# A job's scaled result leaves behind the next branch, and the short job runs its first layer by halves

## The chip, the cores and the metric

The kernel runs on one core of one Trainium2 chip. It uses TensorE (matmuls, into PSUM), VectorE, ScalarE, GpSimd (here mostly to issue gathers and scatters by a list of row numbers) and SyncE (which issues the plain DMA loads). The metric is the device time of one execution in microseconds. Every engine has its own queue of instructions and its own sequencer; the engines wait for each other by semaphores, and at a branch in the program each engine compares and jumps for itself.

## The reference, cut to what matters

Three layers follow each other: attention with a window and some global tokens, a dense layer of three products with a maximum, and a mixture of experts. Only the last is touched:

```python
logits = x @ w_gate                      # 1152 tokens, 8 experts
expert_idx = np.argmax(logits, axis=1)
...
h = np.maximum(np.einsum('ecd,edf->ecf', disp, w1), 0.0)   # 512 -> 1024
y = np.einsum('ecf,efd->ecd', h, w2)                       # 1024 -> 512
...
out[i] = gate_w[i] * y[expert_idx[i], pos[i]]              # at most 288 tokens per expert
```

So every token goes through the two layers of its expert, and its row is scaled by the gate's weight and put at its place in `out`. Rows over the capacity of 288 stay zero.

## The kernel before

The first 265 us compute attention, the dense layer, the routing and the fullest expert (job 0). What is left is cut into **jobs** of at most 128 tokens of one expert, the fullest first. Their number and sizes are known only at run time, so the program is a nest of branches, written by the recursion `jobs` (L1209): job j runs, then a branch (L1214) looks at the count of job j + 1. Over 32 tokens, the next full job follows; else a second branch inside the Else (L1217) either runs the **short job** `small` (L990), for 1 to 32 tokens, or ends. With these inputs four full jobs run (1 to 4), and job 5 is a short one.

A full job (`job`, L984) has 24 matmuls of the first layer (`first_tile`, L890, into two PSUM banks of `ACC`), ScalarE's Relu (L895), four transposes for each of the two halves of the hidden layer (`hidden`, L911, copied out at L912 and L913), and 24 matmuls of the second layer (`second`, L924). In between, by hand-written places, ScalarE and VectorE split the next job's weights into two parts (L840, L841), the next job's tokens are transposed (`xprep`, L811 to L816), the next count is loaded into a register on each engine (L1200), a hint on the coming branch is given (L982), and GpSimd gathers the tokens of the job after next (L799). SyncE loads the weights for the job after next as the splits free their buffers; where such a job doesn't exist, the load moves nothing.

At the end of `second` ScalarE scales the 128 x 512 result by the gate's weights into `y` (L930), and GpSimd scatters `y` to the rows of `out` (L931). Both are written ahead of the branch. All scatters write the same tensor `out`; the framework that orders the instructions makes each of them wait until the one before has landed.

The short job works with weights as they were loaded: `small` has 16 small matmuls for the first layer (L998, four groups of 32 rows, 256 columns each), one Relu by ScalarE (L1003), two transposes (L1005), a copy by VectorE (L1006), eight one-column operations by VectorE that make row numbers and gate weights for four column blocks (L1011, L1012), 32 small matmuls for the second layer (L1017), a scaling by ScalarE (L1019) and a scatter by GpSimd (L1020). After it the program ends: SyncE waits for all DMAs, and the engines meet (L1311).

In the trace a 4-byte matmul of the source shows as two records.

Of the kernel before, what the change touches and what calls it, by code (L numbers as in the profile page):

```python
# [7 lines left out]
F32 = mybir.dt.float32  # L8
# [5 lines left out]
AF = mybir.ActivationFunctionType  # L14
# [5 lines left out]
P = 128  # L20
# [3 lines left out]
DM = H * D  # L24
# [10 lines left out]
NJ = NU_ + 1  # L35
# [15 lines left out]
def tile_block(ctx: ExitStack, tc: tile.TileContext, qk, qg, v, vo, vg, w123, w_out, w_gate, w1, w2, consts, out):  # L51
    nc = tc.nc
# [65 lines left out]
    ident = cst[:, 0:P]  # L118
# [527 lines left out]
    k = 0  # L646
# [8 lines left out]
    ps_x = ctx.enter_context(tc.tile_pool(name="ps_x", bufs=2, space=PSUM))  # L655
    ps_y = ctx.enter_context(tc.tile_pool(name="ps_y", bufs=2, space=PSUM))
# [10 lines left out]
    k = 0  # L667
# [100 lines left out]
    def drive(main, sides=()):  # L768

        t, due = 0, [[g, 0] for g in sides]  # L770
        for _ in main:
            t += 1
            for d in due:
                if d[0] is not None and d[1] <= t:
                    n = next(d[0], None)
                    d[0], d[1] = (None, 0) if n is None else (d[0], t + n)
        for d in due:
            if d[0] is not None:
                for _ in d[0]:
                    pass  # L780

    def chain(*gens):
        for g in gens:
            yield from g() if callable(g) else g
# [7 lines left out]
    TOK = [(0, P), (P, P), (2 * P, CAP - 2 * P)]  # L792
# [25 lines left out]
    XS = []  # L818
# [5 lines left out]
    def raw_of(j, k):  # L824

        r = rw0[k % 3] if j == 0 and k < 5 else raw2[k]
        return r if k < 4 else r.rearrange("p (i f) -> p i f", i=2)
# [87 lines left out]
    def second(j, t, a0):  # L915

        hh, hl = H0, H0[:, :, CAP + 32 :]
        _, _, w2h, w2l = WS[j % 2]
        nt = TOK[t][1]
        py = ps_y.tile([P, DM], F32, tag="py", name="py")  # L920
        i = 0
        for a, w_, c0 in ((hh, w2h, 0), (hh, w2l, 0), (hl, w2h, 0), (hh, w2h, 4), (hh, w2l, 4), (hl, w2h, 4)):
            for c in range(c0, c0 + 4):
                nc.tensor.matmul(py[0:nt], lhsT=a[:, c, a0 : a0 + nt], rhs=w_[:, c], start=i == 0, stop=i == 23)  # L924
                i += 1
                if i < 24:
                    yield
        i_ = IDS[j][0:nt, t]
        y = pB.tile([P, DM], F32, tag="y", bufs=2, name="y")
        nc.scalar.mul(y[0:nt], py[0:nt], i_[:, 2:3])  # L930
        nc.gpsimd.indirect_dma_start(  # L931
            out=out, out_offset=bass.IndirectOffsetOnAxis(ap=i_[:, 1:2].bitcast(I32), axis=0),
            in_=y[0:nt], in_offset=None, bounds_check=NT - 1, oob_is_err=False)
        yield


    FEW = 2 * P
# [21 lines left out]
            in_=y[0:32], in_offset=None, bounds_check=NT - 1, oob_is_err=False)  # L959
        yield  # L960

    ACC = [None, None]

    def accumulators():
        a = [ps_mm.tile([P, 512], F32, tag="mm", name=f"acc{i}") for i in range(3)] + [ps_m4.tile([P, 512], F32, tag="mm", name="acc3")]
        ACC[:] = [a[0:2], a[2:4]]

    def tile_of(j, place):

        yield place  # L970
        xprep(j, 0, ps_x, "px")
        gather_tile(j + 2, 0)

    def counts(j, place):

        yield place
        count_of(j)

    def hint(j, place):

        yield place
        tc.mark_branch_hint_location(f"job{j}", nreg[j] > SMALL, [mybir.EngineType.PE, mybir.EngineType.Activation, mybir.EngineType.DVE, mybir.EngineType.Pool])  # L982

    def job(j):  # L984

        more = j + 1 < NJ
        sides = [counts(j + 1, 6), splits(j + 1, ((0, 0), (1, 3), (2, 13), (3, 19), (4, 25), (5, 31), (6, 35), (7, 39))), tile_of(j + 1, 30), hint(j + 1, 20)] if more else []
        drive(chain(first_tile(j, 0, ACC[j % 2]), second(j, 0, 0)), [hidden(P, (18, 28)), *sides])

    def small(j):  # L990

        sx = pB.tile([P, 512], F32, tag="hs", bufs=2, name="sx")
        sh = pB.tile([P, 512], F32, tag="hs", bufs=2, name="sh")
        ph = ACC[j % 2][0]
        for k in range(4):
            for g in range(4):
                r = slice(32 * g, 32 * g + 32)
                nc.tensor.matmul(ph[r, 0:256], lhsT=XS[0][:, k], rhs=raw_of(j, k)[:, 256 * g : 256 * g + 256], start=k == 0, stop=k == 3)  # L998
        hr = sx[:, 0:256]
        hT_ = sh[:, 0:256].rearrange("p (i t) -> p i t", i=2)  # L1000
        pt = ps_x.tile([P, 2, P], F32, tag="px", name="st")
        py = ps_y.tile([P, P], F32, tag="py", name="sy")
        nc.scalar.activation(hr, ph[:, 0:256], AF.Relu)  # L1003
        for i in range(2):
            nc.tensor.transpose(pt[:, i], hr[:, i * P : i * P + P], ident)  # L1005
        nc.vector.tensor_copy(hT_, pt)  # L1006
        i_ = IDS[j][0:SMALL, 0]
        io, g4 = sh[:, 256:257].bitcast(I32), sh[:, 257:258]
        for q in range(4):
            r = slice(32 * q, 32 * q + 32)  # L1010
            nc.vector.tensor_copy(g4[r], i_[:, 2:3])  # L1011
            nc.vector.tensor_scalar(io[r], i_[:, 1:2].bitcast(I32), 4.0, float(q), op0=ALU.mult, op1=ALU.add)  # L1012
        for i in range(2):
            for k in range(4):
                for q in range(4):
                    r = slice(32 * q, 32 * q + 32)
                    nc.tensor.matmul(py[r], lhsT=hT_[:, i, 32 * k : 32 * k + 32], rhs=raw_of(j, 4 + k)[:, i, q * P : q * P + P], start=i == 0 and k == 0, stop=i == 1 and k == 3)  # L1017
        y = pB.tile([P, DM], F32, tag="y", bufs=2, name="ys")
        nc.scalar.mul(y[:, 0:P], py, g4)  # L1019
        nc.gpsimd.indirect_dma_start(  # L1020
            out=out.rearrange("t (q c) -> (t q) c", q=4), out_offset=bass.IndirectOffsetOnAxis(ap=io, axis=0),
            in_=y[:, 0:P], in_offset=None, bounds_check=4 * NT - 1, oob_is_err=False)
# [5 lines left out]
    ereg, nreg, nsp = [None] * NJ, [None] * NJ, [None] * NJ  # L1028
# [75 lines left out]
    def splits(j, places):  # L1104
        t = 0
        for k, p in places:
            yield p - t
            t = p
            split(j, k)
# [82 lines left out]
    def regs(*jobs):  # L1192

        a, b = jobs[0], min(jobs[-1], NJ - 1) + 1
        if a < b:
            for i, (to, top) in enumerate(((ereg, NE - 1), (nsp, NT))):
                _, to[a:b] = nc.values_load_multi_w_load_instructions(order[0:1, i, a - 1 : b - 1], engines=(mybir.EngineType.SP,), min_val=0, max_val=top)
# [11 lines left out]
    def jobs(j):  # L1209
        if j > 1:  # L1210
            regs(j + 2, j + 2)
        job(j)
        if j + 1 < NJ:
            with tc.If(nreg[j + 1] > SMALL, label=f"job{j + 1}") as c:  # L1214
                jobs(j + 1)
            with c.Else():
                with tc.If(nreg[j + 1] > 0):  # L1217
                    small(j + 1)

    drive(  # L1220
        chain(first_wide(0, CAP, ps_w), second(0, 0, 0), second(0, 1, P), second_few(0, 2)),
# [93 lines left out]
```

## Time and profile before

| what | us |
|---|---|
| median of three runs | 329.09 |
| the three runs | 330.13, 329.09, 327.28 |
| the profiled execution | 327.76 |
| its span, from the first to the last instruction | 325.9 |
| TensorE busy in the span | 309.4 (95%) |
| VectorE, ScalarE, GpSimd busy | 230.6, 183.6, 148.3 |

The span is what the profile's rows cover; the device time of the same execution is 1.86 us longer. All times of rows are counted from the span's start. A busy share is a mean over stages with different limits: what a change in one stage is worth is read in that stage.

### The profile page before, as it was taken

What the parts mean: (1) busy time and instruction counts of PE and PEld (TensorE: products, weight loads), DVE (VectorE), ACT (ScalarE), POOL (GpSimd) and SP (SyncE); (2) the same over time, 40 slices, a digit from 0 to 9 for tenths busy, and PEclk for the clock granted to TensorE, in tenths of its full rate; (3) what the DMA queues carried; (4) which work ended last, traced back from release to release, by engine and by line L of the source; (5) the groups of instructions that cost most, each with busy time, mean ns of one, the idle gap of its engine ahead of it and who ended that gap; (6) DMA issues with size and microseconds to landing.
All of it is one profiled execution on the core that took longest, in us unless ns stands there. A gap on an engine that the chain in (4) does not pass through costs nothing. (4 is left out here: it accounts for less than half of the span.)

```text
span 325.9 us, 8459 instructions
## 1 busy us (share of the span) xinstructions
PE 309.4 (95%) x3145; PEld 257.7 (79%) x3145; DVE 230.6 (71%) x593; ACT 183.6 (56%) x470; POOL 148.3 (45%) x164
## 2 busy tenths in 40 slices
PE   7999878999999999999999999999999999999982
PEld 2444646777777899999999999999899777888762
DVE  1668988964768528989996002755878799999881
ACT  2987767868657323343442121346531689889860
POOL 1267789663566704776788000142000447831131
PEclk9999999999999999999999999999999999999999
DMA  7968769490335942234420011479755299999920
GB/s 256 412 229 286 272 213 354 163 349 22 131 143 177 179 121 66 73 124 129 131 64 3 2 64 66 145 258 344 251 167 228 64 329 400 394 404 400 389 70 31
DMA packets 27655, 64.41 MB, mean 198 GB/s; under 512 B 3018, under 2 KB 8140, under 8 KB 27600
## 3 DMA queue, kind: packets, MB, share of 16 engines
q1 hardware_dynamic: 26304, 59.91, 53.3%
q0 software_dynamic: 1296, 3.82, 3.2%
q8 instruction: 28, 0.46, 0.6%
q14 instruction: 27, 0.22, 0.2%
HBM read 60.95 MB, written 7.27 MB: 209 GB/s over the span
## 5 line engine op out<-in xcount | busy, mean ns | idle before, releaser
L439 PE MATMUL h<-xh,wh 128*128 128x256 f32 (+1 forms) x288 | 84.4, 293 | 0.4 <-DVE hA L426 0.4
L439 PE MATMUL h<-xl,wh 128*128 128x256 f32 (+1 forms) x288 | 84.5, 293 | 0.0
L439 PE MATMUL h<-xh,wl 128*128 128x256 f32 (+1 forms) x288 | 84.2, 292 | 0.0
L439 PEld LDWEIGHTS h<-xh,wh 128*128 128x128 f32 x288 | 54.6, 190 | 1.1 <-DVE hA L426 0.6
L439 PEld LDWEIGHTS h<-xl,wh 128*128 128x128 f32 x288 | 54.8, 190 | 0.9 <-issue 0.7
L439 PEld LDWEIGHTS h<-xh,wl 128*128 128x128 f32 x288 | 54.7, 190 | 0.8 <-issue 0.7
L429 POOL TENSOR_TENSOR hTl<-hA,hTh 128x256 fp32r<-128x256 f32 (+1 forms) x24 | 19.3, 805 | 56.5 <-ACT hTh L428 55.7
L428 ACT CAST hTh<-hA 128x256 fp32r<-128x256 f32 (+1 forms) x24 | 10.0, 417 | 34.5 <-DVE hA L426 34.5
L239 POOL CAST xh<-xs 128x128 fp32r<-128x128 f32 x32 | 13.5, 422 | 34.8 <-ACT xs L237 34.8
L721 PE MATMUL x<-hTl,wo_h 128*128 128x256 f32 (+1 forms) x96 | 28.3, 295 | 0.0
L841 DVE TENSOR_TENSOR w2l<-rawb,w2h 128x1024 fp32r<-128x1024 f32 x23 | 27.2, 1216 | 1.4 <-ACT w2h L840 1.4
L721 PE MATMUL x<-hTh,wo_l 128*128 128x256 f32 (+1 forms) x96 | 28.0, 291 | 0.0
L198 ACT ACTIVATE sm<-sm,nm 128x128 f32<-128x128 f32 x64 | 25.2, 398 | 4.9 <-DVE nm L193 4.9
L721 PE MATMUL x<-hTh,wo_h 128*128 128x256 f32 (+1 forms) x96 | 27.8, 290 | 0.0
L426 DVE TENSOR_TENSOR hA<-hA,h 128x256 f32<-128x256 f32 (+1 forms) x48 | 20.7, 432 | 9.9 <-PE h L439 8.5
L340 POOL TENSOR_TENSOR ct<-ct,wh 128x512 f32<-128x512 f32 x18 | 25.6, 1423 | 1.3 <-DVE ca L337 0.8
L924 PE MATMUL py<-w2h,hhl 128*128 128x512 f32 x96 | 25.5, 395 | 0.2 <-DVE idsall L558 0.2
L193 DVE CUSTOM_DVE_ANT_0 sm<-s,mask 128x128 f32<-128x128 f32 x64 | 15.9, 284 | 13.6 <-PE s L179 13.3
L341 POOL TENSOR_TENSOR wl<-ct,ca 128x512 fp32r<-128x512 f32 x18 | 24.3, 1352 | 2.0 <-DVE ca L339 0.7
L841 DVE TENSOR_TENSOR w1l<-rawb,w1h 128x1024 fp32r<-128x1024 f32 x20 | 23.7, 1216 | 1.8 <-ACT w1h L840 1.8
L840 ACT CAST w2h<-rawb 128x1024 fp32r<-128x1024 f32 x23 | 23.4, 1050 | 0.7 <-DMA rawb<-in_w_dram 0.6
L799 POOL DMA_INDIRECT xg<-x2d,idsall x7 | 14.8, 2120 | 16.2 <-PE xp L811 15.0
(230 smaller groups left out, 716.0 us busy)
## 6 DMA issues: line engine op xcount, KB each, us to landing
rawb<-in_w_dram SPq DMA_DIRECT2D x51, 512.0 KB
raww<-in_w_dram SPq DMA_DIRECT2D x18, 512.0 KB
rawv<-in_v_dram SPq DMA_DIRECT2D x16, 512.0 KB
qk<-in_qk_dram SPq DMA_DIRECT2D x16, 320.0 KB
rawo<-in_w_out_dram SPq DMA_DIRECT2D x6, 512.0 KB
rw<-in_w_dram SPq DMA_DIRECT2D x5, 512.0 KB
out_dram<-zero SPq DMA_DIRECT2D x1, 2176.0 KB
rawg<-in_vo_dram SPq DMA_DIRECT2D x4, 512.0 KB
```

The source lines that it names most:

```text
L193: nc.vector.tensor_tensor_reduce(sm[:, j], ps[:, j, 0:P], mk, scale=-0.125, scalar=3.0e38, op0=ALU.add, op1=ALU.min, accum_out=nm[:, j : j ...
L198: nc.scalar.activation(sm[:, j], sm[:, j], AF.Exp, bias=nm[:, j : j + 1], scale=-1.0, accum_out=ssum[:, j : j + 1])
L340: nc.gpsimd.tensor_tensor(tf, tf, hi.bitcast(F32), op=ALU.subtract)
L341: nc.gpsimd.tensor_tensor(lo, tf, b.bitcast(F32), op=ALU.add)
L426: nc.vector.tensor_tensor(hA[:, :T], hA[:, :T], ph[:, :T], op=ALU.max)
L429: nc.gpsimd.tensor_tensor(hl[:, f_, c0 : c0 + T], hA[:, :T], dst.bitcast(F32), op=ALU.subtract)
L439: nc.tensor.matmul(ph[:, :T], lhsT=w_[:, a], rhs=x_[:, c, c0 : c0 + T], start=n == 0, stop=n == 11)
L721: nc.tensor.matmul(po[:, :T], lhsT=w_[:, f, d * P : (d + 1) * P], rhs=h_[:, f_, c0 : c0 + T], start=k == 0, stop=k == 17)
L799: nc.gpsimd.indirect_dma_start(out=xg[t if j == 0 else j % 2], out_offset=None, in_=src, in_offset=bass.IndirectOffsetOnAxis(ap=IDS[j][0:n ...
L840: nc.scalar.copy(h_, raw_of(j, k))
L841: nc.vector.tensor_tensor(l_, raw_of(j, k), h_.bitcast(F32), op=ALU.subtract)
L924: nc.tensor.matmul(py[0:nt], lhsT=a[:, c, a0 : a0 + nt], rhs=w_[:, c], start=i == 0, stop=i == 23)
```

## The change

The last two steps of `second`, the scaling and the scatter, become a function of their own, `leave`. For job 0 it is still called at once. For a full job j it is called at three other places: at the start of job j + 1, behind the branch; in the short job that follows, behind the copies of the transposed hidden layer; or in a new Else when no job follows. The result must then outlive the branch, so the second layer of odd and even jobs writes to two fixed PSUM tiles, `YP`.

In the short job the first layer is done in two halves of 128 columns for each group, into two PSUM banks, with a Relu of each; the two transposes go to two PSUM tiles, and each is copied by ScalarE as it comes (before: one copy by VectorE).

```diff
--- before.py
+++ after.py
@@ -917,7 +917,7 @@
         hh, hl = H0, H0[:, :, CAP + 32 :]
         _, _, w2h, w2l = WS[j % 2]
         nt = TOK[t][1]
-        py = ps_y.tile([P, DM], F32, tag="py", name="py")
+        py = YP[j % 2] if j else ps_y.tile([P, DM], F32, tag="py", name="py")
         i = 0
         for a, w_, c0 in ((hh, w2h, 0), (hh, w2l, 0), (hl, w2h, 0), (hh, w2h, 4), (hh, w2l, 4), (hl, w2h, 4)):
             for c in range(c0, c0 + 4):
@@ -925,13 +925,19 @@
                 i += 1
                 if i < 24:
                     yield
+        if not j:
+            leave(j, t, py)
+        yield
+
+    def leave(j, t, py):
+
+        nt = TOK[t][1]
         i_ = IDS[j][0:nt, t]
         y = pB.tile([P, DM], F32, tag="y", bufs=2, name="y")
         nc.scalar.mul(y[0:nt], py[0:nt], i_[:, 2:3])
         nc.gpsimd.indirect_dma_start(
             out=out, out_offset=bass.IndirectOffsetOnAxis(ap=i_[:, 1:2].bitcast(I32), axis=0),
             in_=y[0:nt], in_offset=None, bounds_check=NT - 1, oob_is_err=False)
-        yield
 
 
     FEW = 2 * P
@@ -959,11 +965,12 @@
             in_=y[0:32], in_offset=None, bounds_check=NT - 1, oob_is_err=False)
         yield
 
-    ACC = [None, None]
+    ACC, YP = [None, None], [None, None]
 
     def accumulators():
         a = [ps_mm.tile([P, 512], F32, tag="mm", name=f"acc{i}") for i in range(3)] + [ps_m4.tile([P, 512], F32, tag="mm", name="acc3")]
         ACC[:] = [a[0:2], a[2:4]]
+        YP[:] = [ps_y.tile([P, DM], F32, tag="py", name=f"yp{i}") for i in range(2)]
 
     def tile_of(j, place):
 
@@ -991,19 +998,22 @@
 
         sx = pB.tile([P, 512], F32, tag="hs", bufs=2, name="sx")
         sh = pB.tile([P, 512], F32, tag="hs", bufs=2, name="sh")
-        ph = ACC[j % 2][0]
-        for k in range(4):
-            for g in range(4):
-                r = slice(32 * g, 32 * g + 32)
-                nc.tensor.matmul(ph[r, 0:256], lhsT=XS[0][:, k], rhs=raw_of(j, k)[:, 256 * g : 256 * g + 256], start=k == 0, stop=k == 3)
         hr = sx[:, 0:256]
         hT_ = sh[:, 0:256].rearrange("p (i t) -> p i t", i=2)
-        pt = ps_x.tile([P, 2, P], F32, tag="px", name="st")
-        py = ps_y.tile([P, P], F32, tag="py", name="sy")
-        nc.scalar.activation(hr, ph[:, 0:256], AF.Relu)
+        pt = [ps_x.tile([P, P], F32, tag="px", name=f"st{i}") for i in range(2)]
+        py = YP[j % 2][:, 0:P]
         for i in range(2):
-            nc.tensor.transpose(pt[:, i], hr[:, i * P : i * P + P], ident)
-        nc.vector.tensor_copy(hT_, pt)
+            ph = ACC[j % 2][i]
+            for k in range(4):
+                for g in range(4):
+                    r = slice(32 * g, 32 * g + 32)
+                    a = 256 * g + i * P
+                    nc.tensor.matmul(ph[r, 0:P], lhsT=XS[0][:, k], rhs=raw_of(j, k)[:, a : a + P], start=k == 0, stop=k == 3)
+            nc.scalar.activation(hr[:, i * P : i * P + P], ph[:, 0:P], AF.Relu)
+        for i in range(2):
+            nc.tensor.transpose(pt[i], hr[:, i * P : i * P + P], ident)
+            nc.scalar.copy(hT_[:, i], pt[i])
+        leave(j - 1, 0, YP[(j - 1) % 2])
         i_ = IDS[j][0:SMALL, 0]
         io, g4 = sh[:, 256:257].bitcast(I32), sh[:, 257:258]
         for q in range(4):
@@ -1209,13 +1219,19 @@
     def jobs(j):
         if j > 1:
             regs(j + 2, j + 2)
+        if j > 1:
+            leave(j - 1, 0, YP[(j - 1) % 2])
         job(j)
-        if j + 1 < NJ:
+        if j + 1 == NJ:
+            leave(j, 0, YP[j % 2])
+        else:
             with tc.If(nreg[j + 1] > SMALL, label=f"job{j + 1}") as c:
                 jobs(j + 1)
             with c.Else():
-                with tc.If(nreg[j + 1] > 0):
+                with tc.If(nreg[j + 1] > 0, label=f"few{j + 1}") as d:
                     small(j + 1)
+                with d.Else():
+                    leave(j, 0, YP[j % 2])
 
     drive(
         chain(first_wide(0, CAP, ps_w), second(0, 0, 0), second(0, 1, P), second_few(0, 2)),
```

How this moves the instructions is shown at three places. In these rows a name in brackets is a semaphore: PE, Activation and DVE count instructions of those engines, DMASW numbers are counted up by GpSimd's DMAs when they have landed, and DMAHW numbers by SyncE's.

ScalarE at the end of job 4, before: the last two casts of job 5's weights, then the scaling, then the branch.

```order
L840 CAST w2h_3749<-rawb 128x1024 [waits DMAHW4_49]
L840 CAST w2h_3749<-rawb 128x1024 [waits DMAHW5_49]
L930 ACTIVATE y<-py,idsall 128x512 [waits DMASW4_49,PE_49]
L1214 COMPARE_AND_BRANCH
L840 CAST w1h_3440<-rawb 128x1024 [waits DMAHW6_49]
```

The same place in the changed kernel (the last two rows belong to a full job 5).

```order
L840 CAST w2h_3749<-rawb 128x1024 [waits DMAHW4_49]
L840 CAST w2h_3749<-rawb 128x1024 [waits DMAHW5_49]
L1228 COMPARE_AND_BRANCH
L937 ACTIVATE y<-yp_4230,idsall 128x512 [waits DMASW4_49,PE_49]
L840 CAST w1h_3440<-rawb 128x1024 [waits DMAHW6_49]
```

The scaling has moved past the branch, and nothing else has moved.

ScalarE in the short job 5, before: Relu and the final scaling.

```order
L1217 COMPARE_AND_BRANCH
L1003 ACTIVATE sx<-acc_4228 128x256 [waits PE_49,Activation_49]
L1019 ACTIVATE ys<-sy,sh 128x128 [waits DMASW6_49,DVE_49,PE_49]
L1217 UNCONDITIONAL_BRANCH [waits Activation_sequencer_49]
```

The same short job in the changed kernel.

```order
L1231 COMPARE_AND_BRANCH
L1012 ACTIVATE sx<-acc_4228 128x128 [waits PE_49,Activation_49]
L1012 ACTIVATE sx<-acc_4229 128x128 [waits PE_49]
L1015 COPY sh<-st_7625 128x128 [waits PE_49]
L1015 COPY sh<-st_7626 128x128 [waits PE_49]
L937 ACTIVATE y<-yp_4230,idsall 128x512 [waits DMASW4_49]
L1029 ACTIVATE ys<-yp_4231,sh 128x128 [waits DMASW6_49,DVE_49,PE_49]
L1231 UNCONDITIONAL_BRANCH [waits Activation_sequencer_49]
```

Job 4's scaling (L937) now stands between the copies and the final scaling.

GpSimd, before: the end of job 4 (gather, scatter, branch).

```order
L799 DMA xg_3437<-x2d,idsall 128x512 [waits DMASW3_49,PE_49]
L931 DMA out_dram<-y,idsall 1088x512 [waits DMASW6_49,Activation_49]
L1214 COMPARE_AND_BRANCH
```

GpSimd, before: the short job 5. Its scatter waits for DMASW0, which in the trace is the semaphore that job 4's scatter counts up.

```order
L1217 COMPARE_AND_BRANCH
L1311 ISA [waits DMASW1_49]
L1020 DMA out_dram<-ys,sh 4352x128 [waits DMASW0_49,DVE_49,Activation_49]
```

GpSimd in the changed kernel: the short job 5 holds both scatters.

```order
L1231 COMPARE_AND_BRANCH
L1327 ISA [waits DMASW0_49]
L938 DMA out_dram<-y,idsall 1088x512 [waits DMASW6_49,Activation_49]
L1327 ISA [waits DMASW1_49]
L1030 DMA out_dram<-ys,sh 4352x128 [waits DMASW0_49,DVE_49,Activation_49]
```

Job 4's scatter has moved past the branch to right ahead of the short job's own scatter, whose waits are the same as before.

## Rows read from the trace of the kernel before

**Rows 1.** Busy time by stretch: third and fourth full job, then the end.
```profile
core 0: us, PE busy (x) PEld busy (x) DVE busy (x) ACT busy (x) POOL busy (x), PEclk, DMA share, GB/s
289.80:302.27 12.47, 12.47 (x61) 10.13 (x61) 11.48 (x13) 11.35 (x15) 2.49 (x2) 1.00 1.04 400
302.27:314.92 12.65, 12.65 (x61) 9.97 (x59) 11.60 (x13) 10.98 (x14) 2.58 (x2) 1.00 0.73 267
314.92:325.90 10.98, 4.33 (x99) 2.82 (x98) 2.63 (x11) 1.44 (x3) 2.30 (x2) 0.98 0.09 27
```
**Rows 2.** Timeline of TensorE in the short job: start, length, what [idle before <-releaser].
```profile
314.92 1.93 PE L998 MATMUL acc<-rawb,x 128*32 128x256 f32 x32
318.43 0.44 PE L1005 MATMUL st<-cst,sx 128*128 128x128 f32 x2 [1.57 <-ACT sx L1003]
319.45 1.95 PE L1017 MATMUL sy<-rawb,sh 128*32 128x128 f32 x64 [0.59 <-DVE sh L1006]
```
**Rows 3.** Timeline of ScalarE, from the end of job 3 on.
```profile
302.48 0.69 ACT L930 ACTIVATE y<-py,idsall 128x512 f32<-128x512 f32 x1 [0.47 <-PE py L924]
303.06 1.98 ACT L840 CAST w1h<-rawb 128x1024 fp32r<-128x1024 f32 x2
...
311.55 2.94 ACT L840 CAST w2h<-rawb 128x1024 fp32r<-128x1024 f32 x3
315.03 0.69 ACT L930 ACTIVATE y<-py,idsall 128x512 f32<-128x512 f32 x1 [0.53 <-PE py L924]
317.99 0.38 ACT L1003 ACTIVATE sx<-acc 128x256 f32<-128x256 f32 x1 [2.27 <-issue]
321.47 0.37 ACT L1019 ACTIVATE ys<-sy,sh 128x128 f32<-128x128 f32 x1 [3.10 <-PE sy L1017]
```
**Rows 4.** Source views of both branches, 311 to 326: ns min/median/max, first and last start.
```profile
L1214 PEldq COMPARE_BRANCH  x1: 467/467/467, 312.3 to 312.3; - x1
L1214 ACTq COMPARE_BRANCH  x1: 73/73/73, 315.0 to 315.0; - x1
...
L1217 PEldq COMPARE_BRANCH  x2: 65/1729/3393, 312.8 to 320.7; - x2
L1217 DVEq COMPARE_BRANCH  x2: 47/52/57, 317.6 to 319.6; - x2
L1217 ACTq COMPARE_BRANCH  x2: 38/44/50, 317.8 to 321.5; - x2
```
**Rows 5.** Timeline of VectorE in the short job: the copy, first and last of eight.
```profile
318.97 0.42 DVE L1006 COPY sh<-st 128x256 f32<-128x256 f32 x1 [2.56 <-PE st L1005]
319.31 0.13 DVE L1011 COPY sh<-idsall 32x1 f32<-32x1 f32 x1
...
320.02 0.14 DVE L1012 TENSOR_SCALAR sh<-idsall 32x1 int32<-32x1 int32 x1
```
**Rows 6.** Timeline of GpSimd at the end: job 4's scatter and the last one.
```profile
316.00 1.30 POOL L931 DMA_INDIRECT out_dram<-y,idsall  x1 [3.50 <-ACT y L930]
322.12 0.99 POOL L1020 DMA_INDIRECT out_dram<-ys,sh  x1 [4.82 <-POOLq L1214]
```
**Rows 7.** Source views, landings: all six L931; job 4's; L1020; gather L799 at 311.3.
```profile
DMA to landing us min/median/max: 2.8/6.5/8.0
...
DMA to landing us min/median/max: 3.5/3.5/3.5
...
L1020 POOLq EVENT_SEMAPHORE  x1: 637/637/637, 319.6 to 319.6; - x1
...
DMA to landing us min/median/max: 2.2/2.2/2.2
...
L799 POOL DMA_INDIRECT xg<-x2d,idsall x1: 1191/1191/1191, 311.3 to 311.3; - x1
...
DMA to landing us min/median/max: 4.2/4.2/4.2
```
**Rows 8.** Source view of L930, 300 to 326: its waits in ScalarE's queue.
```profile
L930 ACTq EVENT_SEMAPHORE  x2: 17/17/17, 300.6 to 311.8; - x2
```
**Rows 9.** Groups by line, attention: ScalarE's copy of 128 x 128 out of PSUM.
```profile
L237 ACT COPY xs<-pxq 128x128 f32<-128x128 f32 x32 | 8.5, 266 | 5.7 <-PE pxq L234 5.0
```

## Prediction: what the change does to the time

> **What bounds the kernel now.** I read the busy time by stretch first. In the four full jobs, from 264.77 to 314.92 us, TensorE is busy for the whole of each stretch (12.47 us in the shortest, 12.65 in the longest), so nothing on another engine can shorten them [rows 1]. In the last stretch, 10.98 us, it is busy 4.33 us: that is the short job and the end of the program, the only place where a change of order can give time back [rows 1]. So I followed that end with the timeline of each engine.
>
> TensorE does the short job's first layer from 314.92 for 1.93 us, to 316.85 [rows 2]. ScalarE's Relu starts only at 317.99, and what ended ScalarE's idle time is "issue", not TensorE [rows 3]. The branch rows say why: ScalarE's sequencer makes the first compare (L1214) at 315.0, with job 4's scaling (L930), and arrives at the next compare, inside the Else (L1217), at 317.8. It takes 2.8 us to get there; TensorE, which passed the branch at 312.3, takes 0.5 [rows 4]. So 317.99 - 316.85 = 1.14 us of the end are ScalarE's late arrival. From there it is a chain: Relu to 318.37, two transposes to 318.87, VectorE's copy 318.97 to 319.39, TensorE's second layer 319.45 to 321.40, ScalarE's scaling 321.47 to 321.84, GpSimd's scatter at 322.12 [rows 2, 3, 5, 6]. That scatter lands 2.2 us after it starts, at 324.3 [rows 7], and the span ends at 325.9, 1.6 us later.
>
> One row matters more than it seems to: before the last scatter, GpSimd's queue stands in a semaphore wait from 319.6 for 637 ns [rows 7]. In the order of the instructions L1020 waits for DMASW0, which job 4's scatter counts up: both write `out`. Job 4's scatter (L931) started at 316.00 [rows 6] and landed 3.5 us later [rows 7], at 319.5, just where that wait's record begins. Today this wait costs nothing, since VectorE ends at 320.16 [rows 5] and ScalarE at 321.84.
>
> **The change, part by part.** *The branch is moved ahead of the scaling.* At the end of job 4 ScalarE's queue had L930's first wait behind it at 311.8 [rows 8], two casts before it could run, so the sequencer runs ahead of the engine and stood at L930 until TensorE was done. Without L930 it meets the branch at about 311.8; 2.8 us later, at 314.6, it is in the short job, ahead of TensorE's first half. The 1.14 us go. If the branch were taken only when the last cast ends (311.55 + 2.94 = 314.49 [rows 3]), arrival would be 317.3; that is a rival below.
>
> *In jobs 2 to 4* the moved pair (one scaling of 0.69 us, one scatter of 1.3 us) stands right behind the branch instead of right ahead of it, on ScalarE ahead of the same casts, on GpSimd ahead of the same register load. It waits for the same last matmul, and there the branch falls through (a cast at 303.06 follows the scaling of 302.48 without a gap [rows 3]). Cost 0, hidden by TensorE's full stretches; without that cover 3 x 0.69 = 2.1 us. On SyncE and its loads nothing moves. The fixed PSUM tiles yp0/yp1 alternate as the two buffers did before; job 5 uses the one that job 3's scaling read at 302.48: no wait. The new Else (count zero) isn't executed.
>
> *The first layer by halves.* 32 records of 256 columns take 1.93 us; the second layer's 64 of 128 columns take 1.95 [rows 2]. The halves are 64 of 128 columns, so I take 1.95: half 0 ends at about 315.9, half 1 at 316.87. A Relu of 128x128 isn't in the trace; it lies between the 128x128 PSUM copy, 0.27 us, and the 128x256 Relu, 0.38 [rows 9, 3]. I take 0.27, the same tile size. Relu 0 is done long before half 1. With the steps between engines as rows 2, 3 and 5 have them (0.07 to ScalarE, 0.06 to TensorE): Relu 1 316.94 to 317.21, transpose 1 317.27 to 317.57 (a pair took 0.44, one of it 0.30), ScalarE's second copy 317.64 to 317.91. The first copy is done by 317.4, so the second layer starts behind the transposes at 317.55 and ends at 319.5 (its second half needs the copy of 317.91 only at 318.5). That is 1.9 us before today's 321.40.
>
> *VectorE loses its copy* (0.42 us). Its eight small operations run from 317.6, when its branch is through [rows 4], for 0.85 us (319.31 to 320.16 today [rows 5]); they are done at 318.5, before anyone needs them.
>
> *Job 4's scaling and scatter, inside the short job.* They are written behind the second copy: ScalarE 317.91 to 318.60, under the second layer; the final scaling behind it needs TensorE until 319.5 and runs 319.57 to 319.94. GpSimd started 0.28 us after ScalarE in both scatters (315.72 to 316.00, 321.84 to 322.12 [rows 3, 6]), so job 4's scatter starts at 318.9 instead of 316.00. That is 2.9 us later, and what is queued behind it on GpSimd is the last scatter, which waits for its landing. With 3.5 us it lands at 322.4, and the last scatter starts at about 322.7. Today it starts at 322.12. **The sum: +0.6 us.** The 1.9 us that TensorE and ScalarE gain end in a wait for a DMA. From there 2.2 and 1.6 us follow as before.
>
> The unknown is that landing. All six of L931 lie between 2.8 and 8.0 us, median 6.5, and the gather just ahead took 4.2 [rows 7]; the long ones fell into stretches with a DMA share above 1.0, the end has 0.09 [rows 1]. So I take 3.5, the one measured in this place. With 2.8 the sum is -0.1, with 4.2 +1.3, and with Relus and copies at 0.38 three times 0.11 more: own range -0.1 to +1.6.
>
> [...] The trace has 3.5 us for job 4's 128 x 512 f32 [rows 7]. [...]
>
> **The rivals.**
> *A. The gain arrives* (the last scatter doesn't stand behind job 4's landing). It starts 0.28 us after 319.94, at 320.22, GpSimd being free of job 4's scatter at 318.9 + 1.3 = 320.2: -1.9 us. For it: TensorE and ScalarE do get there. Against: the wait on DMASW0 stands in the order of both kernels, and a landing within 1.1 us would be needed, where the shortest is 2.8.
> *B. A short landing*, as the shortest row, 2.8: the last scatter at 318.9 + 2.8 + 0.28 = 322.0, -0.1 us. For it: less is in flight than at 316. [...] Against: the one row of this place.
> *C. The branch isn't hidden:* ScalarE arrives at 317.3, Relu 0 at 317.45, Relu 1 behind it until 317.99; everything from Relu 1's end on shifts by 0.78: +1.4 us, slower than before. It decides from the point where ScalarE arrives after 316.7 (316.94 less one Relu). Against: the early semaphore row of L930 [rows 8].
> *D. A loaded landing*, 6.5 us, the median: the last scatter at 325.7, +3.6 us. Any landing over 2.9 us (322.12 - 0.28 - 318.9) makes it slower than before. Against: the DMA engines are nearly empty there.
>
> **How the numbers follow.** Forecast (held by the landing, about +0.6) 0.65; B 0.14; A 0.09; C 0.07; D 0.05. The profiled execution took 327.76 us, 1.86 more than its span; with +0.6 it would be 328.4. The median of the three runs, 329.09, lies 1.33 above it, and the four executions go from 327.28 to 330.13, so their spread is larger than the effect. I put the +0.6 on their mean, (330.13 + 329.09 + 327.28 + 327.76) / 4 = 328.6: **329.2 us**. The likeliest case alone gives 328.5 to 330.2; C at the top (330.0) and B at the bottom (328.5) lie in or by it, and 1.1 us at the lower end and 0.9 at the upper for the spread make **327.4 to 331.1**. A (326.7) and D (332.2) are left out, 0.14 together. One per cent, 3.3 us, is about what a measurement of this kernel can tell from no change. Only D passes it (0.05); A doesn't, but with the spread I leave 0.04 for faster: faster 0.04, within one per cent 0.91, slower 0.05.
>
> **What would show it.** Right: the first Relu's idle time ends with TensorE's accumulator, not with "issue"; the second layer starts at about 317.5 and ends at 319.5; job 4's scatter starts near 318.9; GpSimd idles from about 320.2 and starts the last scatter near 322.7, 2.8 us after ScalarE's scaling. Wrong: the last scatter at 320.2 (A); the first Relu again behind "issue" (C); job 4's landing far from 3.5 us (B, D). A TensorE stretch of the full jobs that isn't full would break the step that costs them at nothing.

## The result and the profile after

| | before | after |
|---|---|---|
| median (us) | 329.35, 8 runs, 327.28 to 332.19 | 330.94, 8 runs, 329.58 to 332.46 |
| profiled execution, its span (us) | 327.76, 325.9 | 331.47, 329.7 |

The ratio is 1.0068, 95% interval 1.0039 to 1.0097: the change makes the kernel slower by 0.68%, some 2.2 us. That is inside the range and inside one per cent, but it is a loss that can be measured, where the sum on record had +0.6 us.

Busy time by stretch in the kernel after, for the same three stretches as in [rows 1]:

```profile
core 0: us, PE busy (x) PEld busy (x) DVE busy (x) ACT busy (x) POOL busy (x), PEclk, DMA share, GB/s
290.30:302.80 12.50, 12.50 (x62) 10.15 (x61) 11.45 (x13) 11.03 (x14) 2.53 (x2) 1.00 1.04 401
302.80:315.45 12.65, 12.65 (x61) 9.97 (x59) 11.61 (x13) 10.98 (x14) 2.58 (x2) 1.00 0.72 255
315.45:329.70 14.25, 4.82 (x131) 3.78 (x130) 2.30 (x10) 2.02 (x6) 2.01 (x2) 0.84 0.07 20
```

TensorE is busy for the whole of these full jobs, as before. Most of the loss is in the last stretch: 14.25 us, where it was 10.98. The short job starts at 315.45, where it was 314.92. Of these 0.53 us, 0.42 lie in job 2, from its first matmul to job 3's (the first row is of before, the second of after):

```profile
277.32:289.86 12.54, 12.54 (x61) 10.16 (x60) 12.11 (x14) 10.72 (x14) 7.83 (x3) 1.00 1.03 399
277.43:290.39 12.96, 12.95 (x62) 10.08 (x60) 12.01 (x14) 11.10 (x14) 8.65 (x3) 1.00 1.04 399
```

In the ten other kernels below job 2 takes 12.53 to 12.56 us, also in the eight whose scalings of jobs 1 to 3 are moved in the same way, so this was seen in one execution only. In the ten the short job starts between 314.37 and 318.01. So from here on times are counted from the first matmul of the short job, and the end of the span, so counted, is called the **tail**: 10.99 us before, 14.24 after.

TensorE in the short job, beside [rows 2]; then its waits in this stretch, by line:

```profile
315.45 0.85 PE L1011 MATMUL acc<-rawb,x 128*32 128x128 f32 x21
317.94 1.50 PE L1011 MATMUL acc<-rawb,x 128*32 128x128 f32 x43 [1.64 <-issue]
319.37 0.77 PE L1014 MATMUL st<-cst,sx 128*128 128x128 f32 x2
320.07 1.95 PE L1027 MATMUL yp<-rawb,sh 128*32 128x128 f32 x64
```
```profile
POOL out_dram L938 <- ACT y L937: 8.3, 1, 8.3
ACT sx L1012 <- PE acc L1011: 4.2, 2, 3.7
POOL out_dram L1030 <- POOLq L1228: 3.4, 1, 3.4
PEld acc L1011 <- issue: 2.3, 2, 1.9
```

The first layer takes 3.99 us (315.45 to 319.44), not 1.95. After 21 records TensorE stands for 1.64 us, and what ended the idle time is "issue": nothing that the profile shows. Its weight loads stop too (1.9 us). Such a gap is in no row of before.

ScalarE, beside [rows 3]:

```profile
318.69 0.28 ACT L1012 ACTIVATE sx<-acc 128x128 f32<-128x128 f32 x1 [3.66 <-PE acc L1011]
319.48 0.28 ACT L1012 ACTIVATE sx<-acc 128x128 f32<-128x128 f32 x1 [0.52 <-PE acc L1011]
319.74 0.27 ACT L1015 COPY sh<-st 128x128 f32<-128x128 f32 x1
320.18 0.27 ACT L1015 COPY sh<-st 128x128 f32<-128x128 f32 x1 [0.17 <-PE st L1014]
320.34 0.69 ACT L937 ACTIVATE y<-yp,idsall 128x512 f32<-128x512 f32 x1
322.09 0.37 ACT L1029 ACTIVATE ys<-yp,sh 128x128 f32<-128x128 f32 x1 [1.06 <-PE yp L1027]
```

The first Relu now waits for TensorE's accumulator, not for "issue". The source views of the two branches, beside [rows 4], say why: ScalarE makes the first compare at 312.4 and is at the second at 315.0, before TensorE begins.

```profile
L1228 ACTq COMPARE_BRANCH  x1: 73/73/73, 312.4 to 312.4; - x1
...
L1231 ACTq COMPARE_BRANCH  x2: 38/44/50, 315.0 to 322.2; - x2
```

GpSimd, beside [rows 6], and the source views of its two scatters, beside [rows 7]:

```profile
321.31 1.02 POOL L938 DMA_INDIRECT out_dram<-y,idsall  x1 [8.29 <-ACT y L937]
325.71 0.99 POOL L1030 DMA_INDIRECT out_dram<-ys,sh  x1 [3.38 <-POOLq L1228]
```
```profile
DMA to landing us min/median/max: 3.6/3.6/3.6
...
L1030 POOLq EVENT_SEMAPHORE  x1: 43/43/43, 324.9 to 324.9; - x1
...
DMA to landing us min/median/max: 2.4/2.4/2.4
```

ScalarE is done with the final scaling at 322.46, but the last scatter starts 3.25 us later, at 325.71. In between GpSimd waits: job 4's scatter started at 321.31, landed 3.59 us later at 324.90, the semaphore record stands at 324.9, and another 0.81 us pass until the scatter starts.

So there were two readings to test. **F**: the gap in the first layer is TensorE waiting for its own instructions, and depends on where in the program the short job's code stands. Its rivals: the gap comes with the halves (two PSUM banks, twice as many instructions), or with data that are late. **S**: the last scatter stands behind the landing of job 4's scatter. Its rival: GpSimd's own queue is slow there for another reason.

### The profile page after: what moved, and what is told of

The parts are those of the page before. It is cut to its first block, busy times and chain, and to the rows that moved or that the text cites. A ratio compares the mean times of both kernels' runs of the same rounds, so it can differ in the third digit from the quotient of the medians.

```text
span 329.7 us, 8524 instructions
## 1 busy us (share of the span) xinstructions
PE 309.9 (94%) x3177; PEld 258.4 (78%) x3177; DVE 230.0 (70%) x592; ACT 184.2 (56%) x473; POOL 149.1 (45%) x164
## 5 line engine op out<-in xcount | busy, mean ns | idle before, releaser
L799 POOL DMA_INDIRECT xg<-x2d,idsall x7 | 14.8, 2121 | 15.8 <-PE xp L811 14.6
L840 ACT CAST w1h<-rawb 128x1024 fp32r<-128x1024 f32 x20 | 20.3, 1046 | 1.6 <-DMA rawb<-in_w_dram 1.6
```

The source lines that it names most:

```text
L799: nc.gpsimd.indirect_dma_start(out=xg[t if j == 0 else j % 2], out_offset=None, in_=src, in_offset=bass.IndirectOffsetOnAxis(ap=IDS[j][0:n ...
L840: nc.scalar.copy(h_, raw_of(j, k))
```

## The experiments

Four kernels were timed in rounds against the kernel before (e1, e4, e6 and e11, 12 executions each); the others ran once and are read by their tails. A tail is that of one execution: by it the kernel after loses 3.25 us and e1 2.29, in the timed runs 2.2 and 1.1. So the tails tell what waits for what, and a price only to about 1 us. All times in this table are counted from the first matmul of the short job, from the timelines and landings of each kernel.

| kernel | first layer ends (gap behind record) | second layer ends | job 4's scatter, start to landing | last scatter, start to landing | tail |
|---|---|---|---|---|---|
| before | 1.93 (none) | 6.48 | 1.07 to 4.62 | 7.19 to 9.36 | 10.99 |
| after | 3.99 (21) | 6.57 | 5.86 to 9.45 | 10.26 to 12.61 | 14.24 |
| e1_moved_code | 1.96 (none) | 4.56 | 3.85 to 8.27 | 9.07 to 11.65 | 13.28 |
| e9_code_moved_24 | 5.14 (9) | 8.26 | 7.16 to 10.91 | 11.72 to 14.39 | 16.02 |
| e5_before_code_moved | 3.71 (21) | 7.24 | 1.07 to 4.40 | 7.96 to 10.12 | 11.75 |
| e8_halves_only | 3.61 (21) | 6.26 | 1.07 to 5.13 | 6.97 to 9.14 | 10.77 |
| e7_no_job4_scatter | 3.83 (21) | 6.41 | none | 7.12 to 9.33 | 10.92 |
| e3_scatter_first | 3.88 (21) | 6.47 | 1.99 to 6.00 | 7.18 to 10.10 | 11.73 |
| e4_first_and_moved | 1.95 (none) | 4.56 | 1.12 to 4.35 | 5.28 to 8.54 | 10.18 |
| e6_first_full_width | 1.93 (none) | 5.62 | 1.12 to 4.18 | 6.33 to 9.46 | 11.09 |
| e10_first_moved_no_job4_scatter | 1.95 (none) | 4.57 | none | 5.28 to 8.11 | 9.70 |
| e11_first_and_moved_110 | 1.95 (none) | 4.57 | 1.12 to 4.35 | 5.28 to 8.45 | 10.08 |

### F: the place of the code

**e1_moved_code** is the kernel after with 32 transposes more in the short job of the last possible job. That block isn't run with these inputs, but it stands in the program ahead of the one that is. A transpose is two instructions of TensorE (the short job's two are two weight loads and two matmuls in the trace of after), so the executed code stands 64 instructions further back, and nothing else differs.

```diff
+        for _ in range(32 if j == NJ - 1 else 0):
+            nc.tensor.transpose(pt[0], ident, ident)
         i_ = IDS[j][0:SMALL, 0]
```

> The changed kernel, with 32 transposes more (64 TensorE instructions) in the short job of job 16, which is never executed; it only moves the code of job 5's short job by 64 instructions. Theory F (TensorE's gap of 1.64 us in the first layer is the fetch of the next piece of its program, and it falls there because of where the code stands): no gap, the 64 records of the first layer in about 1.95 us, the last scatter starts 8.2 us after the layer's first matmul (10.26 in the changed kernel, 7.20 before), about 1.0 to 1.3 us slower than before. Rival H (the gap belongs to the layer in halves, its second bank or its weights): the gap stays at about 1.6 us and the last scatter at 10.3.

TensorE's timeline in e1:

```profile
315.20 1.96 PE L1011 MATMUL acc<-rawb,x 128*32 128x128 f32 x64
317.08 0.80 PE L1014 MATMUL st<-cst,sx 128*128 128x128 f32 x2
317.81 1.95 PE L1029 MATMUL yp<-rawb,sh 128*32 128x128 f32 x64
```

The gap is gone: 64 records in one piece, 1.96 us, and the second layer ends 4.56 us after the first matmul (4.58 predicted). The time is 329.82 us against 328.76, ratio 1.0033 (1.0004 to 1.0061). So instructions that never run take off about half of the loss; the two intervals overlap, so it is the profile that shows the gap's removal, and the ratio only agrees. What remains, S has to explain.

**e9_code_moved_24** is the same with 12 transposes, 24 instructions.

```diff
+        for _ in range(12 if j == NJ - 1 else 0):
+            nc.tensor.transpose(pt[0], ident, ident)
```

> The changed kernel with 12 transposes (24 TensorE instructions, 12 weight loads and 12 matmuls) more in the never executed short job. Theory F, with a border in the program that has moved 24 instructions nearer: the gap comes after 9 or 10 records instead of 21 and ends at the same time, about 2.5 us after the first matmul, so it is about 0.3 us longer; first layer done at 4.3 us. Rival H: gap after 21 records as before.

TensorE's timeline in e9:

```profile
314.84 0.51 PE L1011 MATMUL acc<-rawb,x 128*32 128x128 f32 x9
317.44 2.54 PE L1011 MATMUL acc<-rawb,x 128*32 128x128 f32 x55 [2.08 <-issue]
```

The gap has come 12 records nearer, from behind record 21 to behind record 9: 12 pairs of weight load and matmul are the 24 instructions. It is a fixed place in the program at which TensorE stops, not a place in the data or in the halves.

The gap is longer too, 2.08 us, but that isn't all of the tail of 16.02: the first layer ends at 5.14, where 4.3 was expected. The rest of the first layer, the transposes and the second layer (columns as in [rows 1]):

```profile
317.44:319.98 2.54, 2.54 (x56) 2.14 (x55) 0.82 (x8) 0.28 (x1) 0.00 (x0) 0.65 0.06 16
319.91:320.83 0.92, 0.92 (x9) 0.44 (x10) 0.00 (x0) 0.54 (x2) 0.00 (x0) 0.50 0.03 9
320.76:323.10 2.34, 2.34 (x65) 2.00 (x64) 0.00 (x0) 0.85 (x2) 1.02 (x1) 0.82 0.02 7
```

After it had stood for 2.08 us, TensorE's granted clock fell to 0.50, 0.75 us behind the gap's end and for 3.4 us. In the kernel after, with its gap of 1.64 us, it stays at 1.00 to the end of the second layer. At the pace of the kernel after (43 records in 1.50 us) the 55 records would take 1.92 us, so by this estimate the clock costs 0.62 us there, 0.15 in the transposes (0.92 for 0.77) and 0.39 in the second layer (2.34 for 1.95).

**e5_before_code_moved** moves the code of the kernel *before*, by 96 such transposes.

```diff
+        for _ in range(96 if j == NJ - 1 else 0):
+            nc.tensor.transpose(pt[:, 0], ident, ident)
```

> The kernel before, with 96 transposes (192 TensorE instructions) more in the never executed short job of job 16, so that job 5's short job stands in TensorE's program where the changed kernel has it. Theory F (the gap is the fetch at a fixed place of the program): a gap of 1 to 1.6 us after about 21 of the 32 records, first layer done about 3.4 us after its first matmul; since ScalarE comes at 3.1 there anyway, the last scatter only moves from 7.2 to about 7.5. Rival H (the gap belongs to the halves): no gap, 1.93 us, 7.2.

TensorE's timeline in e5:

```profile
315.92 1.49 PE L998 MATMUL acc<-rawb,x 128*32 128x256 f32 x21
318.57 1.05 PE L998 MATMUL acc<-rawb,x 128*32 128x256 f32 x11 [1.17 <-issue]
```

The gap is now in the kernel before, with its full-width first layer: the rival "it comes with the halves" falls. The first layer ends 1.78 us later, but the tail is only 0.76 us longer (11.75 against 10.99), since ScalarE's late arrival hid the rest. (The layer's end was expected at 3.4 and is at 3.71, the last scatter at 7.5 and is at 7.96.) The single time is 329.44 us.

**What is waited for.** In the view of DMA traffic of the kernel after, from just ahead of the first matmul to the end of the gap, q8, one of the two queues that bring instructions, moves one packet:

```profile
q8 instruction: 1, 0.02, 2.7%
```

The trace's records have this packet of 16 KB at 0.12 us after the first matmul; it took 1.10 us. Every kernel of the table has one there, between -0.59 and +0.20. In the six kernels with the gap TensorE goes on between 2.2 and 2.5 us after that packet's start (after 2.37, e9 2.53, e5 2.45, e8 2.21, e3 2.39, e7 2.50), whether it had stopped behind record 9 or 21. In all twelve kernels the packet starts 1.4 to 2.0 us after TensorE's second compare. That is how a wait for this packet would look: the end is set by the packet, and the place of the stop by the code. But the link is inferred, not shown: the trace doesn't name the packet's contents, and TensorE goes on only 1.3 to 1.5 us after the packet's end, for which no row has a reason.

### S: the last scatter behind a landing

**e7_no_job4_scatter** is the kernel after without job 4's scatter; its scaling stays, and job 4's rows of the output stay zero. `leave` gets a flag for it:

```diff
-        leave(j - 1, 0, YP[(j - 1) % 2])
+        leave(j - 1, 0, YP[(j - 1) % 2], False)      # False: no scatter
```

> The changed kernel without job 4's scatter (its rows of the output stay zero; its scaling is kept). Theory S: the last scatter starts 0.28 us after ScalarE's last scaling, at about 7.3 us after the first matmul, with the gap of 1.6 us still in it. Rival (the 0.8 us from the landing to the last scatter, and the rest, are GpSimd's own): it stays over 9.

ScalarE's last row in e7, and GpSimd's only scatter:

```profile
323.81 0.37 ACT L1030 ACTIVATE ys<-yp,sh 128x128 f32<-128x128 f32 x1 [1.06 <-PE yp L1028]
```
```profile
324.45 1.03 POOL L1031 DMA_INDIRECT out_dram<-ys,sh  x1 [9.54 <-POOLq L1229]
```

ScalarE is done at 324.18, and the scatter starts 0.27 us later. With TensorE's gap still in it, the last scatter starts 3.14 us earlier in the tail than in the kernel after (7.12 against 10.26). The wait was for job 4's scatter. This run takes the scatter out of GpSimd's queue too; e3 keeps it there. And in the three kernels where the last scatter comes behind the landing, it keeps its distance to it while the landing varies: 0.81 us behind a landing of 3.59 (after), 0.80 behind one of 4.42 (e1), 0.81 behind one of 3.76 (e9).

**e3_scatter_first** keeps the work and moves `leave` to the front of the short job, behind the branch, ahead of the first layer.

```diff
     def small(j):
 
+        leave(j - 1, 0, YP[(j - 1) % 2])
         sx = pB.tile([P, 512], F32, tag="hs", bufs=2, name="sx")
...
-        leave(j - 1, 0, YP[(j - 1) % 2])
         i_ = IDS[j][0:SMALL, 0]
```

> The changed kernel, with job 4's scaling and scatter written at the front of the short job instead of behind the copies. Theory S (the last scatter is held by the landing of job 4's scatter): job 4's scatter starts about 1.1 us after the first layer's first matmul and lands by 4.7; the last scatter follows ScalarE's scaling after 0.28 us, at about 7.3 us from the first matmul, with TensorE's gap still there (the code stands where it stood). Rival (GpSimd's branch or its own work holds the last scatter, not the landing): it stays near 10.3.

Job 4's scatter starts at 1.99 instead of 5.86, lands at 6.00, and the last one starts at 7.18, 0.27 us after ScalarE's scaling, 3.1 us earlier than in the kernel after and where it stood before (7.19). So the rival on GpSimd's queue falls. (The start was expected at 1.1 and the landing by 4.7: here ScalarE took 3.2 us from the first compare to the second, 2.6 in the kernel after, and so came to the scaling 0.9 us late. It delayed nothing.) All that the halves and the branch gain is then eaten by the gap alone. The single time is 328.03 us.

**e4_first_and_moved** has both edits, e3's and e1's.

> Both: job 4's scaling and scatter at the front of the short job, and the 64 instructions in the unexecuted short job. Theories F and S together: no gap, second layer done 4.6 us after the first matmul, last scatter at 5.3 us (7.20 before): 1.9 us faster than before. If only S holds: 7.3, as before. If only F holds: about 8.2.

TensorE, ScalarE and GpSimd in e4, and the landing of its last scatter:

```profile
315.18 1.95 PE L1012 MATMUL acc<-rawb,x 128*32 128x128 f32 x64
317.06 0.80 PE L1015 MATMUL st<-cst,sx 128*128 128x128 f32 x2
317.79 1.95 PE L1029 MATMUL yp<-rawb,sh 128*32 128x128 f32 x64
```
```profile
315.33 0.69 ACT L937 ACTIVATE y<-yp,idsall 128x512 f32<-128x512 f32 x1 [0.58 <-PE yp L924]
316.38 0.28 ACT L1013 ACTIVATE sx<-acc 128x128 f32<-128x128 f32 x1 [0.36 <-PE acc L1012]
```
```profile
316.30 1.27 POOL L938 DMA_INDIRECT out_dram<-y,idsall  x1 [3.53 <-ACT y L937]
320.45 1.00 POOL L1032 DMA_INDIRECT out_dram<-ys,sh  x1 [2.89 <-POOLq L1230]
```
```profile
DMA to landing us min/median/max: 3.3/3.3/3.3
```

Scaling at the front delays no Relu: it ends at 316.02 and the Relu waits for TensorE until 316.38. The last scatter starts at 5.28, 1.91 us earlier than before. The time is 327.53 us against 328.76, ratio 0.9965 (0.9941 to 0.9989): faster than before, and by an interval that doesn't touch e1's. Between e1 and e4 only the place of `leave` differs; by the ratios (1.0033 and 0.9965) it is worth 0.68%, 2.2 us.

But 1.91 us were gained at the scatter's start and only 0.81 arrive in the tail (10.18 against 10.99): the last scatter takes 3.27 us to land, where it took 2.17.

### The other runs

**e8_halves_only** has the halves and ScalarE's copies, with the scaling and the scatter ahead of the branch as before. Against the kernel before, cut:

```diff
-        nc.scalar.activation(hr, ph[:, 0:256], AF.Relu)
...
-        nc.vector.tensor_copy(hT_, pt)
+            ph = ACC[j % 2][i]
...
+            nc.scalar.activation(hr[:, i * P : i * P + P], ph[:, 0:P], AF.Relu)
...
+            nc.scalar.copy(hT_[:, i], pt[i])
```

> The other half alone: the first layer by halves and ScalarE's copies, with the scaling and the scatter ahead of the branch as before. Theory F: the gap is there, as in the changed kernel (the code stands in the same place), Relu of the second half at 4.0, second layer done at 6.6, last scatter at 7.3 us after the first matmul, 0.1 later than before; job 4's scatter starts at 1.1 and holds nothing up. So the moved scatter alone would account for the rest up to 10.3.

TensorE and ScalarE in e8:

```profile
315.14 0.85 PE L1004 MATMUL acc<-rawb,x 128*32 128x128 f32 x21
317.25 1.50 PE L1004 MATMUL acc<-rawb,x 128*32 128x128 f32 x43 [1.26 <-issue]
```
```profile
318.43 0.63 ACT L1005 ACTIVATE sx<-acc 128x128 f32<-128x128 f32 x2 [2.50 <-PE acc L1004]
```

The gap is there again, so this run can't tell what the halves alone are worth without it. With it, the tail is 10.77, 0.2 us shorter than before. The single time is 327.69 us. The first Relu starts 1.18 us behind the gap's end, where the kernel after has 0.75 (318.69 less 317.94). ScalarE, which meets the branch behind the scaling, is still late for the first half, though the row names TensorE; its second compare is at 318.3, just ahead of the Relu:

```profile
L1219 ACTq COMPARE_BRANCH  x2: 38/44/50, 318.3 to 321.5; - x2
```

**e6_first_full_width** is the other part alone: `leave` at the front of the short job, with the first layer at full width and VectorE's copy.

```diff
+        leave(j - 1, 0, YP[(j - 1) % 2])
...
+        ph = ACC[j % 2][0]
...
+                nc.tensor.matmul(ph[r, 0:256], lhsT=XS[0][:, k], rhs=raw_of(j, k)[:, 256 * g : 256 * g + 256], start=k == 0, stop=k == 3)
...
+        nc.vector.tensor_copy(hT_, pt)
```

> The change without its second half: job 4's scaling and scatter move behind the branch, to the front of the short job; the first layer stays at full width with one Relu and VectorE's copy, so TensorE's program is that of the kernel before. Theories F and S: no gap; Relu at 2.0 us after the first matmul instead of 3.07 (ScalarE is there early), VectorE's copy at 3.0, second layer done at 5.4, last scatter at 6.1 (7.2 before): about 1.0 us faster, somewhat less if the landing is longer. If ScalarE's early branch were not what freed the Relu: 7.2.

GpSimd in e6, and the landing of the last scatter:

```profile
321.76 0.99 POOL L1028 DMA_INDIRECT out_dram<-ys,sh  x1 [3.94 <-POOLq L1226]
```
```profile
DMA to landing us min/median/max: 3.1/3.1/3.1
```

The last scatter starts 0.86 us earlier than before (6.33 against 7.19), which is the branch's part of the gain (1.14 were expected), but it lands 3.12 us later. The time is 328.32 us against 328.77, ratio 0.9979 (0.9949 to 1.0009): no difference that can be measured.

**The late landing** was then tested twice. The two theories: two scatters close to each other, or the scatter meets TensorE's own fetch of instructions for the jump at the program's end (a packet on q8 starts 0.29 us after the end of the second layer in before, 0.37 in after; whose instructions it holds is not shown). e10 takes job 4's scatter out of e4 (its rows stay zero), e11 is e4 with 55 transposes instead of 32, which moves the code by another 46 instructions.

```diff
-        leave(j - 1, 0, YP[(j - 1) % 2])
+        leave(j - 1, 0, YP[(j - 1) % 2], False)      # e10
...
-        for _ in range(32 if j == NJ - 1 else 0):
+        for _ in range(55 if j == NJ - 1 else 0):     # e11
```

> e4 (scaling and scatter at the front of the short job, 64 unexecuted TensorE instructions) without job 4's scatter; the scaling stays, job 4's output rows are left zero. In e4 the last scatter started 5.28 us after the first matmul of the short job, as early as wanted, but took 3.27 us to land where it took 2.17 in the kernel before. Theory 'two scatters' (the second one of a block lands late because the first is not long gone): without the first one the landing is 2.2 us again and the span ends about 1.1 us earlier behind the first matmul (9.1 instead of 10.18). Theory 'fetch' (the landing meets TensorE's own fetch of instructions for the jump at the program's end, which starts when its second layer ends): nothing changes, 3.0 to 3.3 us, end at about 10.2.

> [...] No gap in the first layer (1.95 us), last scatter 5.3 us after the first matmul, as in e4. [...] Theory 'two scatters': landing 3.0 to 3.3 us as in e4, end at 10.2, ratio about 0.9965.

e10's last scatter starts at 5.28 and lands 2.83 us later: between the two forecasts, and so for neither theory alone. It does show that the lateness isn't only job 4's scatter. e11's lands 3.17 us after its start, within 0.1 of e4: moving the code by 46 instructions did nothing that the profile can tell from e4. Its time is 327.82 us against 328.85, ratio 0.996 (0.9926 to 0.9994): the same gain as e4, measured a second time. In the trace of e4 two packets of instructions come on q8 around that scatter, where before has one; the first of these rows is e4's, from 319.0 to 322.6, the second before's, from 320.7 to 324.3:

```profile
q8 instruction: 2, 0.03, 5.5%
```
```profile
q8 instruction: 1, 0.02, 1.9%
```

But e6 lands late (3.12) with one. Two things that the trace's records add: a landing is the last of 16 increments of a semaphore, and in all twelve kernels at least 12 of the last scatter's 16 are there after 2.2 us; late are the last one (after, e1, e9, e3, e6), two (e10), three (e11) or four (e4). And the packet on q8 that is under way just after the scatter's start takes 1.44 to 2.19 us in the five kernels that land after 2.8 us or more, and 0.93 to 1.41 in the seven others. No run shows which of the two delays the other, or whether a third thing delays both. The cause of this 0.7 to 1.1 us stays open.

## Why the prediction was wrong

**What failed is one term, the first layer by halves.** "The halves are 64 of 128 columns, so I take 1.95" priced the execution of the instructions alone. It measured 3.99 us (e1, without the gap: 1.96). The execution was priced rightly and the stop in it was missing: TensorE stands at a fixed place of its program (e1, e9, e5), and the change moved the short job's code so that this place fell 21 records behind a jump. That TensorE waits there for its own instructions is inferred, not shown. Neither the profile of before nor any row of it could tell the size; the branch rows [rows 4] did show that engines lose up to 2.8 us in getting from one compare to the next, and that should have opened a rival on TensorE.

**The second is a small step: 0.28 us from release to the scatter's start.** That is measured from ScalarE's scaling [rows 3, 6], and e7 shows it again (0.27). When GpSimd waits for a landing instead, it is 0.81 (after), 0.80 (e1), 0.81 (e9). The sum should have had 0.53 us more; with it, +1.1 us would have been forecast for a kernel without the gap, and e1's ratio is 0.33%, 1.1 us. That agreement is loose: e1's interval goes from 0.1 to 2.0 us, and its profiled run, where job 4's landing took 4.42 us, has 2.29 in the tail.

**The rest of the chain came out.** In times after the first matmul:

| step | predicted | after | e1 |
|---|---|---|---|
| first layer's end | 1.95 | 3.99 | 1.96 |
| second layer's start | 2.63 | 4.62 | 2.61 |
| job 4's scatter | 3.98 | 5.86 | 3.85 |
| its landing takes | 3.5 | 3.59 | 4.42 |
| last scatter starts | 7.78 | 10.26 | 9.07 |

From 7.78 to 10.26 are 2.48 us: 1.88 that the gap leaves at job 4's scatter, 0.09 of landing and 0.53 of the start behind it (2.50). The last scatter's landing gives 0.18 more. Against before, the last scatter starts 3.07 us later (10.26 against 7.19) and the tail is 3.25 longer; 0.6 of this was forecast. In the timed runs it is 2.2 us: by the three ratios -1.2 for the gain with nothing in its way (e4), +2.2 for the place of the scatter (e1 less e4), +1.2 for the place of the code (after less e1; their intervals overlap, so by the times alone this part is not clear of the noise).

**The mechanism that decided the forecast, the wait for job 4's landing, is right** (e7, e3), and so are ScalarE's early branch, a Relu of 128 x 128 (0.28 for 0.27), and the full jobs, which stay full (but for the 0.4 us of job 2 in one execution). VectorE was through its branch later than forecast (its eight small operations run from 318.66 to 319.53), and still 2.5 us before the final scaling.

**The rivals.** A (the gain arrives) has the right size for the wrong kernel: its -1.9 us is what e4's last scatter gains, once `leave` is at the front. C (the branch isn't hidden) is out: the first Relu waits for TensorE. B and D asked how long job 4's landing is. In the kernel after it is 3.59, but over the ten kernels with that scatter it goes from 3.06 (e6) to 4.42 (e1): a single row of 3.5 needed bounds about as wide as the 2.8 to 4.2 that it got, with the short end never met and the long one once passed.

The measured median lies in the range and within one per cent because the range was made from the spread of the runs; that is luck as far as the sum goes. The sum was too small, +0.6 where 2.2 us were measured, and its own range, -0.1 to +1.6, doesn't reach it.

## What to carry to other kernels

A moved instruction moves what waits for it: a transfer that nobody waited for (3.5 us of landing under other work) became the end of the chain when its start moved past the cover, so after moving a DMA ask who waits for its *landing* and put it as early behind the branch as its data allow. Behind a branch, an engine's instructions can have a price of their own that no row of the kernel before shows (1.64 us of standing TensorE in the kernel after); a gap that is ended by "issue" in the middle of equal matmuls is tested by moving the code with instructions that never run. And a gain at the start of the last transfer is not yet a gain of the span (in e4 1.91 us at the start, 0.81 in the tail): read its landing too.

## What the runs showed of the hardware

- TensorE stood 1.2 to 2.1 us in the middle of a row of equal matmuls behind a taken branch, at a place that follows the code: 24 instructions inserted in a block that never runs moved it by 12 records, 64 removed it.
- After a stop of 2.08 us (e9) TensorE's granted clock was 0.50 for 3.4 us, and the 64 records of the second layer took 2.34 us for 1.95.
- From the compare of the first branch to that of the second ScalarE took 2.5 to 3.3 us in the twelve kernels, TensorE 0.5 to 1.4.
- The last scatter started 0.80 to 0.81 us after the landing that it waited for (after, e1, e9), and 0.27 to 0.28 us after ScalarE's scaling where it waited for that (before, e3, e7).
- The landing of a 128 x 512 f32 scatter in this quiet end took from 3.06 to 4.42 us. The 32-row one took 2.2 in before, e5, e7 and e8, 2.35 to 2.7 in after, e1 and e9, and 2.8 to 3.3 in the kernels whose chain ahead of it is shortest or where job 4's scatter stands at the front (e3, e4, e6, e10, e11). What is late are the last one to four of its 16 increments; why is open.
